# A new order string for the attention and Fourier part of a fused float32 kernel

## The chip, the cores and the metric

The kernel runs on one core of one Trainium2 chip. The metric is the device time of one execution in microseconds; three runs of the kernel before have a median of 1200.18 us (1198.98 to 1201.79). The profile is of one further execution.

The engines are TensorE (PE, matrix products and transposes; its weight loads are shown as PEld), VectorE (DVE), ScalarE (ACT), GpSimd (POOL) and SyncE (SP, which here only issues DMAs). [...]

## The reference

Two blocks follow each other. The first is attention with random features (8 batches, 8 heads, 576 positions, head size 64, 128 features), the second mixes by a Fourier transform and has an MLP:

```python
def phi(x):
    proj = np.einsum('bhsd,md->bhsm', x, omega)
    sq = np.sum(x * x, axis=-1, keepdims=True) / 2.0
    h = proj - sq
    h = h - np.max(h, axis=-1, keepdims=True)
    return np.exp(h) / np.sqrt(m)
q_p, k_p = (phi(q_s), phi(k_s))
kv = np.einsum('bhsm,bhsd->bhmd', k_p, v)
z = np.sum(k_p, axis=2)
num = np.einsum('bhsm,bhmd->bhsd', q_p, kv)
den = np.einsum('bhsm,bhm->bhs', q_p, z)[..., None] + 1e-06
...
X = np.fft.fft(x, axis=1)
X = np.fft.fft(X, axis=2)
u = x + np.real(X)
un = (u - mean(u)) / np.sqrt(var(u) + 1e-06)
ch = np.maximum(un @ w_ch1, 0.0) @ w_ch2
return u + ch
```

Rows are the 8 x 576 = 4608 positions, of width 512; the MLP is 512 to 2048 to 512. The two MLP weights come as float64, everything else as float32.

## The kernel before

The program has two parts, each listed by a call of `listing.run`: the first at L1188, the second at L1514. The change touches the first alone.

**What the first part does.** Attention goes over 32 pairs of heads (`attn`, from L554), three of them in flight. For a pair, SP loads k and q (`kq`, L375 and L378) and v (`vd`, L383). PE transposes `kq` (L504), ACT evicts the transposes (`kqT`, L514), PE multiplies with the features in quarters of its array (L586), DVE takes the maximum (`nmx`, L530), ACT the exponential (`e`, L547). Then PE forms k'v (L620, 36 products), DVE or ACT evicts it (`kv`, L634 or L636), PE transposes the q features (L504 again, with `e`), ACT evicts them (`qeT`, L521), PE multiplies by `kv` (L667, L675), and DVE divides (L684, L685, L696) or ACT does (L692). An L620, L667 or L586 matmul takes PE only 18 to 35 ns, a transpose some 120 ns, so equal times of PE hold very different numbers of instructions.

After four pairs a batch is complete and is mixed (`mix`, from L708): DVE or POOL fold the rows (L723 to L759), PE multiplies by the tables (L779, L789), ACT evicts (`y`, L802), PE multiplies again (L827, L838), ACT, DVE and POOL form the residual sums (L869, L874, L877, L886, L887), and SP stores them in a scratch tensor `us` (L901; a mirrored half goes out by L857 and is copied back by L912, which waits for both L857 transfers to land).

Beside this run the conversion of the weights from float64 (`raw` loads L468 through four buffers; L436 or L438, L441 to L448, L454), the MLP of the first four row tiles (`plain`: norm L951 to L965, first layer L1021, `ht` L1005 or L1007, second layer L1044, L1057) and the sums of weights and rows that the second part needs (L1114, L1172, L1089; stores L1137, L1139).

**What the second part does.** The remaining 4096 rows go through the MLP in eight blocks of 512, with Strassen-like products: L1228 for the first layer, L1407 for the second. The first L1228 starts at 441 us of the profiled execution.

**What sets the order.** Each piece of work is a generator that yields a `Step` (engine or a choice of engines, an assumed duration, what it needs and frees) and then writes its instructions. `Listing.run` (L184) keeps a list `todo` of the pieces whose next step waits to be listed. Without a string it takes the step that its own clock lets begin first. With the string `PICKS` (L63) each character names the place in `todo` to take next:

```python
pick = next(picks, None)
other, n = divmod(DIGITS.index(pick), 36) if pick else (0, 0)
best = None
for item in todo if pick is None else [todo[n]]:
    got = self.start(*item[2:], other=other)
```

A value of 36 or more (a capital letter or a sign) means the place less 36 and, for a step with a choice, the engine that the listing's clock holds for the second best. So the string decides the order of instructions on all five engines at once, and for a few kinds of steps the engine: L436 POOL or L438 ACT, L454, L723, L739, L752, L886 and L1114 POOL or DVE, L634 DVE or L636 ACT, L696 DVE or L692 ACT, L1005 DVE or L1007 ACT. Buffers, loads on SP and PSUM banks follow the order in which steps are listed.

## Time and profile before

| | |
|---|---|
| median of 3 runs | 1200.18 us |
| the profiled execution | 1200.75 us |
| its span, first to last instruction | 1198.9 us |
| PE busy | 1171.2 us |
| first L1228 matmul (second part) | 441.1 us |
| PE busy from 441 us to 1199 us | 752.2 of 758 us |
| PE clock granted, mean | 0.998 |

How to read the lines that follow in the prediction: the slices cut the span into 40 equal stretches of 30 us, with one digit for each, the busy share in tenths. A wait line says engine, what it was to write and its line, what released it, then us in total, how often, and the longest. "issue" means that nothing with a semaphore held the engine. A line of the timeline has start, duration, engine, line, operation and tile shapes, the number of instructions merged, and in brackets the idle time before. A matmul in float32 stands twice in the profile (L620: 36 in the program, 72 in the trace), a transpose once. q1 is the queue of SP's DMAs, q8 and q14 carry instructions.

### The profile page before, as it was taken

The numbers are of one execution on the slowest core, as the hardware profiler recorded it, in microseconds if no ns is written. First come the engines' busy times: TensorE is split into PE (matmuls) and PEld (weight loads), VectorE is DVE, ScalarE is ACT, GpSimd is POOL, SyncE is SP. The second block draws the span as 40 slices with busy tenths as digits, with TensorE's granted clock in tenths as the row PEclk, the third lists the DMA queues.
The fourth block names the chain that finished last, engine by engine and source line by source line (L and its number), as shares of the span: only waits on it lengthen the run. The fifth ranks groups of instructions, "written<-read, shape, count | busy, mean of one in ns | idle before, by whom it ended". The sixth has DMA issues, their size and how long they took to land.

```text
span 1198.9 us, 31843 instructions
## 1 busy us (share of the span) xinstructions
PE 1171.2 (98%) x12753; PEld 1048.6 (87%) x12753; DVE 702.7 (59%) x1479; ACT 488.6 (41%) x1583; POOL 438.0 (37%) x509
## 2 busy tenths in 40 slices
PE   7899899999999999999999999999999999999998
PEld 6777788878969778998998998999899899899898
DVE  5889888896555652572582473374275176266255
ACT  7989889877755212222222222222222222222211
POOL 3355344553565305304314323322421431431421
PEclk9999999999999999999999999999999999999999
DMA  8655845645663332582482384195096086177155
GB/s 254 184 148 179 244 147 176 205 148 181 176 228 134 121 119 104 187 270 80 147 291 100 105 293 139 63 298 177 13 309 195 30 269 197 62 233 242 62 161 192
DMA packets 144740, 205.71 MB, mean 172 GB/s; under 512 B 49104, under 2 KB 58576, under 8 KB 144592
## 3 DMA queue, kind: packets, MB, share of 16 engines
q1 hardware_dynamic: 144224, 203.54, 53.3%
q8 instruction: 101, 1.65, 0.6%
q14 instruction: 47, 0.39, 0.1%
q10 hardware_dynamic: 368, 0.13, 0.0%
HBM read 171.90 MB, written 35.91 MB: 173 GB/s over the span
## 4 chain that ended last, share of the span: by engine, by line
PE 67%; DVE 0%; issue 0%; ACT 0%; DVEq 0%
PE banks L1228 32%; PE banks L1407 29%; PE banks L1044 2%; PE banks L961 1%; PE banks L1021 1%; PE banks L827 0%; PE banks L779 0%; PE banks L667 0%; PE banks L789 0%; PE banks L838 0%; DVE u L957 0%; DVE part L1387 0%; PE banks L675 0%; ACT qeT L521 0%; DVE ur L1339 0%
## 5 line engine op out<-in xcount | busy, mean ns | idle before, releaser
L1214 DVE CUSTOM_DVE_ANT_0 hid<-banks,s 128x256 f32<-128x256 f32 x192 | 79.7, 423 | 255.3 <-PE banks L1228 250.5
L1407 PE MATMUL banks<-wl,sums 128*128 128x128 f32 x1792 | 217.3, 275 | 0.0
L1407 PEld LDWEIGHTS banks<-wl,sums 128*128 128x128 f32 x1792 | 208.8, 192 | 0.4
L1242 ACT ACTIVATE s<-banks 128x256 f32<-128x256 f32 x192 | 73.7, 384 | 261.1 <-PE banks L1228 261.1
L547 ACT ACTIVATE e<-banks,nmx 128x128 f32<-128x128 f32 x576 | 163.5, 449 | 20.4 <-DVE nmx L530 20.1
L1228 PE MATMUL banks<-unT,w 128*128 128x256 f32 x704 | 167.5, 379 | 0.0
L1228 PEld LDWEIGHTS banks<-unT,w 128*128 128x128 f32 x704 | 132.7, 190 | 17.9 <-issue 0.5
L1382 ACT ACTIVATE s<-banks 128x128 f32<-128x128 f32 x168 | 46.7, 278 | 242.3 <-PE banks L1407 195.7
L1228 PE MATMUL banks<-tt,w1s 128*128 128x256 f32 x512 | 126.2, 379 | 0.0
L1295 POOL TENSOR_TENSOR hs<-hid 128x256 f32<-128x256 f32 x64 | 46.4, 725 | 205.6 <-DVE hid L1214 178.9
L1228 PEld LDWEIGHTS banks<-tt,w1s 128*128 128x128 f32 x512 | 97.2, 190 | 13.3
L530 DVE TENSOR_REDUCE nmx<-banks 128x8 f32<-128x1024 f32 (+1 forms) x96 | 89.8, 954 | 30.4 <-PE banks L586 24.0
L1387 DVE TENSOR_TENSOR part<-banks,s 128x128 f32<-128x128 f32 x168 | 48.9, 291 | 88.9 <-PE banks L1407 88.3
L1407 PE MATMUL banks<-wl,hid 128*128 128x128 f32 x768 | 97.6, 275 | 0.0
L1407 PEld LDWEIGHTS banks<-wl,hid 128*128 128x128 f32 x768 | 93.5, 192 | 1.2
L1295 POOL TENSOR_TENSOR hs<-hid,hs 128x256 f32<-128x256 f32 x64 | 46.6, 729 | 120.1 <-issue 95.2
L521 ACT ACTIVATE qeT<-banks 128x256 f32<-128x256 f32 (+1 forms) x192 | 79.2, 593 | 10.7 <-PE banks L504 10.5
L586 PE MATMUL banks<-om,kqT 64*64 64x128 f32 x2304 | 79.8, 277 | 3.6 <-ACT kqT L514 2.7
L1228 PE MATMUL banks<-unT,w1s 128*128 128x256 f32 x320 | 80.7, 379 | 0.0
L955 POOL TENSOR_TENSOR rstd<-rstd,mhalf 128x1 f32<-128x1 f32 x36 | 25.8, 718 | 142.2 <-DVE rstd L953 141.1
L586 PEld LDWEIGHTS banks<-om,kqT 64*64 64x64 f32 x2304 | 64.5, 134 | 14.3 <-ACT kqT L514 4.1
L1407 PE MATMUL banks<-wl,hs 128*128 128x128 f32 x576 | 74.9, 275 | 0.4 <-DVE part L1387 0.4
(125 smaller groups left out, 1993.2 us busy)
## 6 DMA issues: line engine op xcount, KB each, us to landing
wl<-w2l SPq DMA_DIRECT2D x392, 256.0 KB, 3.7
raw<-in_moe_w_ch_dram SPq DMA_DIRECT2D x32, 512.0 KB, 5.4
kq<-in_k_dram SPq DMA_DIRECT2D x32, 288.0 KB, 3.9
kq<-in_q_dram SPq DMA_DIRECT2D x32, 288.0 KB, 4.4
vd<-in_v_dram SPq DMA_DIRECT2D x32, 288.0 KB, 5.0
u<-us SPq DMA_DIRECT2D x36, 256.0 KB, 4.0
ur<-us SPq DMA_DIRECT2D x36, 256.0 KB, 4.4
out_dram<-ur SPq DMA_DIRECT2D x34, 256.0 KB, 2.4
```

The costliest lines, as they stand in the source:

```text
L521: nc.scalar.activation(out=dst[:, i], in_=of, func=AF.Copy)
L530: nc.vector.tensor_reduce(nmx[:, :, 0:num], pps[:, :, 0 : MF * num].rearrange("p b (c m) -> p b c m", m=MF), axis=AX.X, op=ALU.max, negate ...
L547: nc.scalar.activation(out=e[:, c + (i if num == 1 else 0), :], in_=pps[:, i, MF * c : MF * c + MF], func=AF.Exp, bias=nmx[:, i, c : c + 1],)
L586: nc.tensor.matmul(pps[cols, c, MF * m : MF * m + MF], lhsT=kqT[rows, j, cols], rhs=om2[rows, :],)
L955: nc.gpsimd.tensor_tensor(rstd[:], rstd[:], mhalf[:], op=ALU.pow)
L1214: nc.vector._custom_dve(TENSOR_ADD_SAT, out=o, in0=ps, in1=sb, s0=FMAX, s1=0.0)
L1228: nc.tensor.matmul(ps[:, 0:HT], lhsT=left(dc), rhs=right(dc), start=start and dc == 0, stop=(dc == D2 - 1), skip_group_check=True,)
L1242: nc.scalar.activation(out=s[:], in_=ps[:, 0:HT], func=AF.Copy)
L1295: nc.gpsimd.tensor_tensor(out=o, in0=l, in1=r, op=op)
L1382: nc.scalar.activation(out=s[:], in_=ps[:, 0:128], func=AF.Copy)
L1387: nc.vector.tensor_tensor(out=part[:, t, 128 * m : 128 * m + 128], in0=ps[:, 0:128], in1=saved[with_][:], op=ALU.add,)
L1407: nc.tensor.matmul(ps[:, 0:128], lhsT=left[:, f], rhs=wls[j, i, n][:, f], start=start and f == 0, stop=(f == 3), skip_group_check=True,)
```

## The change

`PICKS` is replaced. Both strings have 1851 characters; the first seven are equal, then they part. 131 characters of the old string and 135 of the new one ask for the second-best engine. Nothing else in the file differs: same steps, same buffers, same assumed durations, same second part.

```diff
 PICKS = (
-    "130ddec4dedefddeef0ebe38dfgabbhi08da9h9h9h928ecigh9bcdgghecbdbgiiegbekl88m7jbcagePOIf7cgig8kk7c87i7j"
...
-    "43b2249ac44b8dH97370bFa24G786CD45777777044224032010"
+    "130ddec0dcd3dedefedeef38dfcfcajjji0j88a88i9i9i827fePhjdgfeiddelghkffhjg8cdikfPiijhcddgiceeffghfeifej"
...
+    "ebf7bGdF7G7743695887a0bJI9F887888477773032113021110"
 )
```

In the built programs every engine's order differs from the first microseconds on. PE still has 6737 matmuls and transposes; up to the first L1228 its instructions come in 372 runs of one line instead of 381. Of the choices of engine, these differ between the two programs (instructions in all):

| operation | before | after |
|---|---|---|
| kv copy, L634 DVE / L636 ACT | 13 / 19 | 18 / 14 |
| division, L696 DVE / L692 ACT (ten each) | 26 / 60 | 27 / 50 |
| ht, L1005 DVE / L1007 ACT | 29 / 35 | 32 / 32 |
| weight cast, L438 ACT / L436 POOL | 17 / 15 | 19 / 13 |
| weight sum, L454 DVE / POOL | 5 / 27 | 7 / 25 |
| fold, L723 DVE / POOL | 10 / 6 | 7 / 9 |
| fold, L752 DVE / POOL | 18 / 14 | 24 / 8 |
| residual, L886 DVE / POOL | 10 / 30 | 11 / 29 |
| w2 sums, L1114 DVE / POOL | 13 / 31 | 16 / 28 |

On SP the loads and stores are the same in kind and number, in another order; for instance, between the second batch's mirror stores (L857) and their copy back (L912) stood three `raw` loads and a k load, and now stands one `raw` load.

## The prediction

> **What bounds the kernel now.** I read the page first (busy times, the slices), then what TensorE (PE) waits for, then PE in order of time at its longest wait, then the DMA queues and the stages there.

> ```profile
> PE 1171.2 (98%) x12753; PEld 1048.6 (87%) x12753; DVE 702.7 (59%) x1479; ACT 488.6 (41%) x1583; POOL 438.0 (37%) x509
> PE   7899899999999999999999999999999999999998
> DVE  5889888896555652572582473374275176266255
> ACT  7989889877755212222222222222222222222211
> DMA  8655845645663332582482384195096086177155
> q8 instruction: 101, 1.65, 0.6%
> ```

> PE is the bound: 1171.2 of 1198.9 us. What is not PE lies in the first eight or nine slices of 30 us, where VectorE (DVE) and ScalarE (ACT) are nearly full too. From 385.6 us to the end the chain of waits is PE after PE. So an order of the first part can win only idle time of PE before about 300 us. The stages price it (columns: stretch, length, busy time and count of PE, weight loads, DVE, ACT, POOL, then PE's clock, DMA share, GB/s):

> ```profile
> 0.00:60.00 60.00, 48.13 (x1195) 40.24 (x1199) 41.24 (x68) 49.93 (x167) 21.93 (x24) 1.00 0.76 219
> 60.00:120.00 60.00, 56.27 (x1196) 47.62 (x1190) 52.93 (x122) 53.50 (x179) 32.46 (x32) 1.00 0.56 163
> 140.40:142.90 2.50, 0.01 (x3) 0.00 (x0) 1.47 (x3) 2.50 (x9) 0.88 (x1) 1.00 1.07 370
> 142.90:147.10 4.20, 4.18 (x44) 4.06 (x45) 2.88 (x7) 1.37 (x4) 1.93 (x2) 0.59 0.93 219
> ```

> Idle PE is 11.9 and 3.7 us in the first two rows and 21.9 us up to 300 us (summed over ten such stretches of 30 us). The releasers:

> ```profile
> PE banks L483 <- DMA om<-in_omega_dram: 4.9, 1, 4.9
> PE banks L620 <- issue: 4.2, 3, 2.5
> PE banks L586 <- ACT kqT L514: 2.7, 5, 1.2
> PE banks L667 <- issue: 1.2, 2, 0.8
> PE banks L504 <- issue: 1.1, 3, 0.7
> ```

> 4.9 us are the first load, which no order removes. 6.5 us are "issue": PE waits for nothing that a semaphore shows. The other 10.5 us are waits for ACT and DVE, and gaps too short to be listed. The longest issue wait, in order of time:

> ```profile
> 137.61 1.72 PE L667 MATMUL banks<-kv,qeT 128*64 128x65 f32 x32
> 139.49 0.92 PE L620 MATMUL banks<-vd,e 64*64 64x65 f32 x46
> 142.92 0.96 PE L620 MATMUL banks<-vd,e 64*64 64x65 f32 x26 [2.51 <-issue]
> 143.81 3.50 PE L504 MATMUL banks<-ident,e 128*128 128x128 f32 x18
> ```

> ```profile
> q1 hardware_dynamic: 1190, 1.77, 101.4%
> q8 instruction: 1, 0.02, 1.3%
> ```

> The wait had a sequel: the clock stood at half from 143.14 to 146.56 us (0.59 in the stage row above), so 18 transposes took 3.50 us instead of about 2.3. Half of 3.41 us, 1.7 us, is the price; it is counted as busy.

> [...] the trace has 3.41 us at half after 2.5 us idle, while idles of 1.17 and 1.14 us did nothing.

> **The change part by part.** Only the order string changes. Same matmuls, same second part; only which step goes next, and for a few steps which engine.

> *PE's blocks.* I counted both built orders into blocks of 256 PE instructions and gave them lengths by this trace's rows (L620: 72 in 1.28 us; L667: 32 in 1.15; L586: 40 in 1.32; transposes about 0.12 each). Stalls before, and what I expect after:
> - 132.00 (1.14): the block grows from 3.65 to 4.30 us. Two mirror stores are still in flight: 0.3.
> - 142.92 (2.51): the block before the wait is now 108 L620 and 20 L667 (1.92 + 0.72 = 2.64 us) against 40 L620, 32 L667, 8 L675, 46 L620 (0.71 + 1.15 + 0.40 + 0.82 = 3.08). Shorter, so worse with the same fetch. But the queue differs. Before, SP issued two 512 KB weight loads at 134.65 and the 512 KB copy back at 136.95, just as the block began (136.9), then q and two v loads. After, one weight load instead of three stands between the mirror stores and the copy, and the copy needs only 100.4 us of PE's and 102.6 of DVE's work before it (104.0 and 107.6 before), so it is mostly through when the block begins at 109.8 us of PE work; the next v load waits for a product inside the block. I take a fetch wait of 1.0 us (bounds 0.4 and 3.6): 1.0 + 2.4 - 2.64 = 0.8; bounds 0.2 and 3.4. At 0.8 the clock stays whole.
> - 166.55 (0.57): 2.45 to 3.76 us, gone. 218.99 (0.21): 4.02 to 4.39, gone.
> - 77.12 (0.84), 39.91 and 34.43 (0.87): lengths within 0.15 us, kept: 0.8 and 0.9. 284.82 (0.33): 4.56 to 4.24, so 0.6.
> - New short blocks: 124 L620 and 4 L586 late in the part (2.3 us; the DMA share there is about 0.37 and fetch waits were mostly 0.2 to 0.7): 0.5. One of 2.83 us (3.02 before, hidden in an ACT wait of 1.17) under denser loads: 0.3.

> Sum after: 0.3 + 0.8 + 0.8 + 0.9 + 0.6 + 0.5 + 0.3 = 4.2, against 6.5 + 1.7 = 8.2: a gain of 4.0. With the bounds of the second line (and the clock at the upper end) it is 4.6 to -0.3.

> *Waits for ACT and DVE.* For each PE group I set the PE work between its trigger and its use against the duration of what lies between (a transpose's eviction at 0.66 us, a maximum of 1.2 us and four exponentials, and so on). The missing time, summed, is 24.4 us before and 22.8 after; 10.5 us were real, so 0.7 gained. Bounds: +2 and -2, since 60 to 90 us looks worse (7.8 to 11.3) and 120 to 210 better. ACT has 3.3 us less to do (5 kv copies at 352 ns, 3 ht at 315, 10 x at 218 less; 2 weight casts at 801 more), which I put in the same 0.7. POOL loses some 11 us and is on no chain.

> *Changes of matmul shape* on PE up to the first L1228: 218 before, 212 after. One costs about 0.1 us (8 L675 start 0.33 us before the next transpose, and 8 of them are 0.22): 0.6 gained.

> *Loads.* The closest load that the new order places is a q load 5.6 us of PE work before its use, behind a v load; before, the closest beside the very first were 4.2 to 6.0 and PE never waited for one. q lands in 4.4 us at the median, v in 5.0. I take nothing; if it is late, 1 to 2 us. Queues of ACT, DVE and POOL: their own fetch packets (8 KB) show some 3.5 us of issue waits together, not PE's; nothing.

> *Second part* (441 us on): PE has 752.2 of 758 there and the order isn't touched; its inputs are ready tens of us ahead by the same counting (DVE 53 us instead of 61 at PE's work of 380): nothing.

> Sum: 4.0 + 0.7 + 0.6 = 5.3 us off the profiled execution's own 1200.75 (span 1198.9 and 1.85 around it): 1195.4. That execution is 0.57 above the median of 1200.18, so against the median 1194.9; I say **1195.0**.

> **Rivals.**
> - *The stall stays* (chance 0.20). The two v products stand back to back, and the fetch is as late as before: 3.63 + 2.4 - 2.64 = 3.4 us, and the clock halves, 1.7. That gives back 2.6 + 1.7 of the 5.3: 1199.7. For it: the shorter block. Against it: the copy moved forward.
> - *Quiet throughout* (0.13): all but 1 us of fetch stalls go, 7.2 + 1.3: 1192.2. For it: only eight places to mend. Against it: five of them keep their block lengths.
> - *DVE becomes the bound* (0.22), the slower side. The new engine choices give DVE 8.2 us more in the first part (5 kv copies 1.4, six folds and their copies 3.8, two weight sums 2.0, three w2 sums 2.3, ht, x and bmp 2.7, less three halves 4.0). At 160 us of PE work the order asks DVE to be 5.8 us of work ahead of PE, instead of 2.5. Between 60 and 270 us DVE is busy 52.93 of the second row's 60 and over 25 of every 30 us on to 270: it has 27 us spare, most of it spent waiting for the matmuls it reduces. If none of that takes up the work, 8.2 - 5.3 = 2.9 us slower: 1203.7. It decides once more than 5.3 of the 8.2 us isn't absorbed. Against it: only 3.3 us of the 8.2 fall before the tightest place.

> **How the numbers follow.** Forecast 0.45, rivals 0.20, 0.13, 0.22. A measurement of this kernel tells about 0.2% (2.4 us) from no change. Forecast: 0.42 faster, 0.03 same. First rival: 0.06 faster, 0.14 same. Second: 0.13 faster. Third: 0.02 same, 0.20 slower. Together 0.61, 0.19, 0.20. The range holds the forecast's terms at their bounds and both near rivals, and leaves out half of the third: 1190.5 to 1202.0. The forecast's own range is 1192 to 1198.

> **What would show it.** In the profile after: issue waits of PE near 4 us instead of 6.5, none over 1.5; no stretch at half clock between 100 and 200 us; PE idle before 300 us near 17 us; ACT and DVE releasers together near 10. It is wrong if an issue wait over 2 us and a half clock remain, if DVE rises above 27 of 30 us between 120 and 240 with PE released by L530, L634 or L696 there, or if anything differs after 441 us beyond a shift.

## The result

| | before | after | ratio |
|---|---|---|---|
| median of 20 runs each | 1199.55 us | 1195.11 us | 0.9967, interval 0.9957 to 0.9978 |
| second series (63 and 22 runs) | 1199.39 us | 1195.88 us | 0.9974, interval 0.9966 to 0.9982 |
| profiled execution | 1200.75 us | 1197.48 us, second series 1196.38 us | |

The new order is faster, by 4.4 and 3.5 us of median in the two series. The page of the kernel after (busy times, the slices of 30 us, the instruction queue):

```profile
PE 1171.4 (98%) x12753; PEld 1048.4 (88%) x12753; DVE 704.6 (59%) x1501; ACT 485.0 (41%) x1567; POOL 427.3 (36%) x494
PE   7999999999999999999999999999999999999998
DVE  4888899886655551572572473474275176266255
ACT  6989899868655112222222222222222222222211
q8 instruction: 101, 1.65, 0.6%
```

PE is busy as long as before (1171.2) and idle for less. The stages (stretch, length, busy time and count of PE, weight loads, DVE, ACT, POOL, then PE's clock, DMA share, GB/s):

```profile
0.00:60.00 60.00, 49.31 (x1174) 41.04 (x1174) 41.04 (x68) 48.17 (x161) 20.51 (x24) 0.97 0.70 203
60.00:120.00 60.00, 56.75 (x1194) 48.38 (x1196) 52.93 (x122) 53.21 (x182) 28.01 (x28) 1.00 0.63 183
24.15:27.56 3.41, 3.41 (x51) 2.96 (x51) 1.55 (x4) 0.00 (x0) 0.53 (x1) 0.50 0.58 157
```

The half clock near 143 us is gone, but this execution has one at 24 us, the third row. PE's releasers up to its first L1228:

```profile
PE banks L483 <- DMA om<-in_omega_dram: 5.0, 1, 5.0
PE banks L667 <- issue: 2.6, 2, 1.9
PE banks L586 <- ACT qeT L521: 2.3, 4, 1.2
PE banks L504 <- ACT e L547: 1.5, 5, 0.4
PE banks L620 <- issue: 1.3, 1, 1.3
PE banks L675 <- issue: 0.7, 1, 0.7
```

And the place that held the stop of 2.51 us before, in order of time:

```profile
138.13 0.80 PE L667 MATMUL banks<-kv,qeT 128*64 128x65 f32 x18
139.64 0.62 PE L667 MATMUL banks<-kv,qeT 128*64 128x65 f32 x14 [0.72 <-issue]
```

PE still stops inside a product (18 of 32 matmuls of L667), at the same place of the 256-instruction count, but for 0.72 us. A second profile of the same kernel has no half clock in the first part; its issue waits:

```profile
PE banks L667 <- issue: 2.1, 2, 1.2
PE banks L620 <- issue: 1.8, 2, 1.3
PE banks L675 <- issue: 1.2, 1, 1.2
```

Where the time came from, up to the first L1228 (idle is that moment less PE's busy time before it):

| us | before | after | after, second profile |
|---|---|---|---|
| first L1228 starts | 440.9 | 437.9 | 436.8 |
| PE idle until then | 22.0 | 18.9 | 19.3 |
| of it the first load | 4.9 | 5.0 | 5.0 |
| of it issue | 6.5 | 4.6 | 5.1 |
| of it ACT, DVE, late loads and short gaps | 10.6 | 9.3 | 9.2 |
| PE busy until then | 418.9 | 419.1 | 417.5 |
| stretch at half clock | 3.41, at 143 us | 3.41, at 24 us | none |

The second profile's gain of 4.1 us is 1.3 of issue, 1.4 of the other waits, and 1.4 of busy time, where the half clock was. The 9.2 us hold 0.6 us in which PE waited for k loads. After the first L1228 nothing changed: 758.0, 757.7 and 757.7 us to the end of the span.

### The profile page after: what moved, and what is told of

Read it like the earlier page. It is cut to its first block, busy times and chain, and to the rows that moved or that the text cites. A ratio compares the mean times of both kernels' runs of the same rounds, so it can differ in the third digit from the quotient of the medians.

```text
span 1195.6 us, 31831 instructions
## 1 busy us (share of the span) xinstructions
PE 1171.4 (98%) x12753; PEld 1048.4 (88%) x12753; DVE 704.6 (59%) x1501; ACT 485.0 (41%) x1567; POOL 427.3 (36%) x494
## 3 DMA queue, kind: packets, MB, share of 16 engines
q8 instruction: 101, 1.65, 0.6%
## 4 chain that ended last, share of the span: by engine, by line
PE 88%; ACT 9%; DVE 1%; issue 1%; DMA 0%; ACTq 0%; DVEq 0%
PE banks L1228 32%; PE banks L1407 29%; PE banks L1021 5%; PE banks L1044 5%; ACT e L547 4%; PE banks L586 4%; PE banks L504 4%; ACT qeT L521 3%; PE banks L667 2%; PE banks L620 2%; PE banks L827 2%; PE banks L961 1%; PE banks L779 1%; ACT kqT L514 1%; PE banks L789 1%
## 5 line engine op out<-in xcount | busy, mean ns | idle before, releaser
L547 ACT ACTIVATE e<-banks,nmx 128x128 f32<-128x128 f32 x576 | 163.3, 453 | 21.9 <-DVE nmx L530 21.7
L1228 PE MATMUL banks<-unT,w 128*128 128x256 f32 x704 | 167.5, 379 | 0.0
L1228 PEld LDWEIGHTS banks<-unT,w 128*128 128x128 f32 x704 | 132.7, 190 | 17.9 <-issue 0.5
L1228 PE MATMUL banks<-tt,w1s 128*128 128x256 f32 x512 | 126.2, 379 | 0.0
L1228 PEld LDWEIGHTS banks<-tt,w1s 128*128 128x128 f32 x512 | 97.3, 190 | 13.2
L530 DVE TENSOR_REDUCE nmx<-banks 128x8 f32<-128x1024 f32 (+1 forms) x96 | 89.4, 952 | 22.8 <-PE banks L586 21.7
L521 ACT ACTIVATE qeT<-banks 128x256 f32<-128x256 f32 (+1 forms) x192 | 82.6, 584 | 14.6 <-PE banks L504 14.1
L586 PE MATMUL banks<-om,kqT 64*64 64x128 f32 x2304 | 80.3, 279 | 3.0 <-ACT qeT L521 2.3
L1228 PE MATMUL banks<-unT,w1s 128*128 128x256 f32 x320 | 80.7, 379 | 0.0
L586 PEld LDWEIGHTS banks<-om,kqT 64*64 64x64 f32 x2304 | 64.6, 135 | 14.2 <-issue 5.2
```

Of the source, the lines that this page charges most:

```text
L521: nc.scalar.activation(out=dst[:, i], in_=of, func=AF.Copy)
L530: nc.vector.tensor_reduce(nmx[:, :, 0:num], pps[:, :, 0 : MF * num].rearrange("p b (c m) -> p b c m", m=MF), axis=AX.X, op=ALU.max, negate ...
L547: nc.scalar.activation(out=e[:, c + (i if num == 1 else 0), :], in_=pps[:, i, MF * c : MF * c + MF], func=AF.Exp, bias=nmx[:, i, c : c + 1],)
L586: nc.tensor.matmul(pps[cols, c, MF * m : MF * m + MF], lhsT=kqT[rows, j, cols], rhs=om2[rows, :],)
L1228: nc.tensor.matmul(ps[:, 0:HT], lhsT=left(dc), rhs=right(dc), start=start and dc == 0, stop=(dc == D2 - 1), skip_group_check=True,)
```

## The experiments

Theory 1: the issue waits are PE waiting for its own next block of 256 instructions. Their size is the time that the block's packet starts late, plus about 2.4 us (an estimate from the kernel before: the packet that starts at 140.55 us takes 1.04 us, and PE goes on 1.33 us after its end), less the work in the block before. By this theory they depend on where block boundaries fall in the order, and on transfers at that moment. Theory 2: they are waits for operands, buffers, ACT or DVE that the trace can't name, and the new order gains because of its better spacing of those. Each ratio is to executions of the kernel before that were timed beside it; the medians are of 5 to 22 executions.

**Moving the boundaries.** Products that nobody reads, ahead of PE's first transposes, where PE waits for its first load. Each is four PE instructions (two matmuls and two weight loads in the trace), so 16, 48 and 64 of them move every boundary by 64, 192 and 256 instructions. Order, waits and buffers stay.

```diff
+        for i in range(16):
+            q = slice(D * (i % 2), D * (i % 2) + D)
+            nc.tensor.matmul(omps[q, 256:257], lhsT=ident[q, q], rhs=ident[q, 0:1])
         nc.tensor.transpose(omps[:, 0:128], om2d, ident[:])
```

The kernel before, moved by 64:

> The kernel before with 16 one-column products (64 PE instructions) ahead of everything, in the time in which PE waits for its first load. Order, buffers and data are those of before; only the grid of 256-instruction blocks lies 64 instructions earlier in the work. Theory 1 (instruction fetch): with a fetch wait of 2 us the blocks of the first part are short by 19.0 us in sum instead of 13.5, so the 8.2 us of fetch stalls and half clock of before should become 10 to 13: slower by 2 to 5 us, and issue waits at other places. Theory 2 (the stops come from data or buffers, and the gain of the new order from ACT and DVE): same places, same time within 1 us.

By 192:

> The same with 48 products (192 PE instructions). Theory 1: the blocks are short by 8.6 us instead of 13.5, so faster by 2 to 4 us, with the long stop near 142.9 us gone or much shorter and no half clock there. Theory 2: no change within 1 us.

By 256, a whole block, as the control:

> The same with 64 products (256 PE instructions): the grid falls on the same instructions as in before, with one block more. A control for what the extra products do by themselves. Theory 1: the same time within 1.5 us (the start of PE may lose up to 1 us[...]) and the stops at the same matmuls as before. Theory 2: no change either.

| kernel before with | median | ratio | first kv product later by |
|---|---|---|---|
| 64 more | 1202.30 | 1.0023, 1.0011 to 1.0035 | 0.6 us earlier |
| 192 more | 1200.21 | 1.0008, 0.9999 to 1.0017 | 1.6 us |
| 256 more | 1202.43 | 1.0027, 1.0017 to 1.0037 | 3.8 us |

The times were half hits. 64 came within its expectation, but its profile is of an execution of 1197.77 us and has 4.6 us of stops at block boundaries and no half clock; so it shows where the stops are, and not what made the median 2.8 us slower. The other two start later, by more than I had allowed for. If that delay passes on in full, which isn't shown, both are some 0.9 us under the kernel before without it, and that isn't the gain that theory 1 expected of 192. The places are what counts. First the control, in order of time, then 64:

```profile
140.87 0.92 PE L620 MATMUL banks<-vd,e 64*64 64x65 f32 x46
145.21 1.13 PE L620 MATMUL banks<-vd,e 64*64 64x65 f32 x26 [3.42 <-issue]
```

```profile
137.04 0.46 PE L620 MATMUL banks<-vd,e 64*64 64x65 f32 x14
138.25 1.14 PE L620 MATMUL banks<-vd,e 64*64 64x65 f32 x58 [0.75 <-issue]
```

Moved by a whole block, PE stops after the same 46 of 72 matmuls as before. Moved by 64, it stops after 14: 32 matmuls with their 32 weight loads earlier, which is 64 instructions. No operand can explain that. With 192 the stop stands in the transposes behind that product:

```profile
142.92 1.58 PE L504 MATMUL banks<-ident,e 128*128 128x128 f32 x13 [2.05 <-ACT w L438]
```

It is listed as released by ACT's weight cast L438, which no transpose of that group reads, and it ends 1.56 us after the block's packet; a name on a stop is no proof.

The new order, moved by 64:

> The changed kernel with 16 one-column products, 64 instructions of TensorE, ahead of its first transposes, where it waits for the first load anyway; they moved the first kv product by less than 0.1 us in the kernel before. Order and waits are otherwise the same; every boundary of an instruction block now lies 64 instructions earlier in the program. Theory 1: the new order was searched for one position of the boundaries, so the stops move to other matmuls and grow: at a fetch wait of 2.0 us the sum of the blocks' shortfalls is 17.7 us instead of 13.7 (a relative measure, not a time), and in the kernel before a rise from 13.5 to 19.0 cost 2.8 us; time +1 to +4 us against the changed kernel, 1196 to 1199. Theory 2: no operand and no buffer comes at another time, so the same within 0.5 us.

It took 1203.05 us (ratio 1.0031, 1.0020 to 1.0042): slower than the kernel before, and 7.2 us slower than the same order without the 16 products, more than I expected. The stop of the last section went from L667 back into L620:

```profile
135.90 2.85 PE L620 MATMUL banks<-vd,e 64*64 64x65 f32 x130
140.25 0.46 PE L620 MATMUL banks<-vd,e 64*64 64x65 f32 x14 [1.50 <-issue]
```

14 matmuls of L620 and 18 of L667 earlier: again 32, and 64 instructions. In this profile the first L1228 starts at 442.36 us instead of 436.83; the stops at block boundaries sum to some 7.9 us (6.4 listed as issue, and one of 1.49 us at 61 us that is listed under L438 and ends 1.38 us after its packet) instead of 5.1 in the second profile, and a half clock of 3.41 us, a price of 1.7, follows the one at 61 us. That is some 4.5 of the 5.5 us; 0.7 more is in waits for ACT (7.9 us instead of 7.2). Moved by 64, the new order (1203.05 us) is no faster than the old one (1202.30 us). So the gain of the new order is tied to one position of the boundaries. The 1.4 us of other waits that it also gained in the second profile have no experiment of their own.

**Changing the transfers.** In the kernel before, three 512 KB transfers were queued ahead of the block that stops at 142.92 us. The first try moved the loads of `raw` 17 and 18 behind the two v loads, and the conversion of `raw` 17, which could not stay ahead of its load; PE's order is the same.

```diff
 SP    raw<-in_moe_w_ch  (16)
-SP    raw<-in_moe_w_ch  (17, 18)
 SP    us<-uh, kq<-in_q, vd<-in_v, vd<-in_v
+SP    raw<-in_moe_w_ch  (17, 18)
 ...
-DVE   L441, L443, L446, L448, L454 of raw 17 as before
+DVE   L441, L443, L446, L448, L454 of raw 17 later
```

> The kernel before with two of its 512 KB weight loads moved behind the two v loads that follow the copy back of the second batch (and the conversion of one of them behind the products, so that nobody waits for it). PE's order and its blocks are exactly those of before. Theory 1: the fetch for the block at 137 us starts 0.5 to 1.5 us after the block begins instead of 3.6, so the stop of 2.5 us shrinks to under 0.8 and the half clock goes: faster by 2 to 4 us. Theory 2: PE's stop stays, within 1 us of before.

It took 1205.12 us, 1.0046 (1.0033 to 1.0058). PE at the target, and 20 us later:

```profile
140.92 0.92 PE L620 MATMUL banks<-vd,e 64*64 64x65 f32 x46
142.21 0.68 PE L620 MATMUL banks<-vd,e 64*64 64x65 f32 x26 [0.37 <-issue]
...
157.56 1.30 PE L586 MATMUL banks<-om,kqT 64*64 64x128 f32 x34
162.90 0.70 PE L586 MATMUL banks<-om,kqT 64*64 64x128 f32 x6 [4.04 <-DVE ht L1005]
```

At the target theory 1 was right: in the packet records the fetch started 1.66 us after PE entered the block before, instead of 3.68, and the stop shrank from 2.51 to 0.37 us, with the clock whole. But the conversion, moved, now stood on DVE's queue ahead of an eviction:

```profile
159.92 2.72 DVE L454 TENSOR_TENSOR w<-w,raw 128x512 f32<-128x512 f32 x1
162.57 0.28 DVE L1005 TENSOR_SCALAR ht<-banks 128x128 f32<-128x128 f32 x1
```

PE waited 4.04 us for that PSUM bank and the clock stood at half for 6.83 us. This is the kind of wait that theory 2 means, and here it was made by hand. So a cleaner try: one load (`raw` 18) behind the v loads, all else in order.

> The kernel before with one load of 512 KB (raw 18) issued on SP's queue behind the two v loads that follow it, and nothing else: all other engines have the same order, which the first try at a quiet window had not kept. Theory 1: the instruction block used at 142.9 us is fetched with 512 KB less ahead of it; its fetch wait falls from 3.6 us to between 1.7 and 3.0, its stop from 2.5 us to between 0.5 and 1.9[...]; time -0.7 to -3.5 us against the kernel before. Theory 2 (operands and buffers): only the v loads come some 1 to 1.5 us earlier and raw 18 later; the stop of 2.5 us keeps its length within 0.3, and the time is the same within 0.5 us unless raw 18's conversion is late.

1198.05 us, 0.9989 (0.9981 to 0.9998). The time is in the range, but not for the stated reason:

```profile
140.78 0.68 PE L620 MATMUL banks<-vd,e 64*64 64x65 f32 x26 [2.00 <-issue]
```

The fetch wait went from 3.68 to 3.26 us only, the stop from 2.51 to 2.00, both outside what theory 1 expected, and the half clock stayed. The first L1228 came 2.3 us earlier in its profile, most of it from other stops and waits. That is inconclusive for the size of the effect.

The opposite on the kernel after: two more transfers, ahead of the copy back, over the block that is used at 140 us. They copy weights to a scratch tensor that nobody reads.

```diff
+            for n in range(2 if b == 1 else 0):
+                nc.sync.dma_start(junk[n], w1v[:, n, 0:CV].bitcast(U32))
             nc.sync.dma_start(*(a.rearrange("p (i d) -> i p d", i=16) for a in (ahead, back)))
```

> The changed kernel with two more transfers of 512 KB, from memory to memory, on SP's queue just ahead of the second batch's copy back (L912), so that transfers lie over the block that is used at 140 us; nothing reads what they write, and TensorE's order is the same. Theory 1: the fetch wait of that block rises from 1.6 us to between 3 and 4, its stop from 0.7 us to between 2 and 3.4[...]; time +2 to +5 us against the changed kernel. Theory 2: the stop stays at 0.7 us or less, since no operand of TensorE comes by these transfers; what could come late are the kq and v loads of later pairs, named in the waits as released by DMA, and without these the time is the same within 1 us.

The kernel after alone, timed beside it:

> The changed kernel once more, for a second profile and for the time beside the next three. Both theories: 1194.5 to 1196.5 us, 3.0 to 5.0 below the kernel before. Theory 1 (the stops of TensorE are waits for its own instruction blocks of 256 instructions) expects the stops at the same places of the instruction order as in the first profile (the blocks used at 24, 63, 140 and 371 us), with sizes that differ by some tenths; the large one at 24 us, with a fetch wait of 4.9 us and a half clock behind it, may be smaller, since that profile was taken at 1197.5 us and most executions lie near 1195. Theory 2 (waits for operands and buffers that the trace puts down as issue) expects the same time and has no opinion on the places.

It took 1195.88 us, with the stops in the places expected, one more of 0.50 us at 134.69 us, and 0.88 us instead of 1.87 at the first. With the transfers 1197.01 us (0.9982, 0.9974 to 0.9990), 1.1 us slower: the stop is in the expected range, the fetch wait and the time are below it, and no half clock followed. The place, in order of time:

```profile
136.63 0.80 PE L667 MATMUL banks<-kv,qeT 128*64 128x65 f32 x18
139.58 0.63 PE L667 MATMUL banks<-kv,qeT 128*64 128x65 f32 x14 [2.15 <-issue]
```

The same matmul, and 2.15 us instead of 0.72 and 1.18; nothing is named as late. The data queue from 136.0 to 139.5 us (packets, MB, share of the 16 engines), with the transfers and then in the first profile of the kernel after:

```profile
q1 hardware_dynamic: 1909, 1.12, 108.2%
```

```profile
q1 hardware_dynamic: 1573, 0.72, 76.7%
```

The fetch wait was 2.65 us here, 1.61 and 1.53 in the two profiles without. Two more kernels that keep this part of the order, the next one and the one with the swap at 59 us, had waits of 1.81 and 1.03 us and stops of 0.85 and 0.20. So the stop with the transfers is longer than in any of four profiles without, and no operand of PE comes by them; theory 2 has no account of it. It is one profile, though, and far from the transfers, at 34.66 us, it has another stop of 1.62 us that neither profile of the kernel after has. Nor does the share of the data queue alone set the wait: between PE's entry into the block before and the start of the packet it was 94% with the transfers, and 89% and 22% in the two profiles without, whose waits are alike.

**Giving the blocks more work.** If, as theory 1 has it, a stop is fetch less work, a slow group between two products of small matmuls removes it. At 371 us, a block of the new order is 124 small matmuls long:

```diff
 L620 x36
+L1021 x4
 L620 x36
-L1021 x4
 L504
```

> The changed kernel with one swap in TensorE's order at 371 us: the projection group L1021 x4 that follows two adjacent kv products (L620, 2 x 36) goes between them. Nothing else is moved but what hangs on the second product. Theory 1: the instruction block that was 124 small matmuls with 1.97 us of work now holds 1.0 us of L1021 as well, 2.8 to 2.9 us; its stop falls from 1.3 us to 0.3 to 0.6, time -0.7 to -1.0 us against the changed kernel. Theory 2: the stop is a wait for an operand or a buffer of the second product, and with one microsecond of other work ahead of it it falls too, but the product then waits for the eviction of the first product's buffer on ScalarE, a wait with ACT as its releaser of up to 0.5 us; time -0.5 to +0.3.

First the kernel after (second profile), then with the swap:

```profile
366.87 2.02 PE L620 MATMUL banks<-vd,e 64*64 64x65 f32 x123
370.21 0.57 PE L620 MATMUL banks<-vd,e 64*64 64x65 f32 x21 [1.32 <-issue]
```

```profile
367.56 1.16 PE L1021 MATMUL banks<-unT,w 128*128 128x128 f32 x8
368.65 0.91 PE L620 MATMUL banks<-vd,e 64*64 64x65 f32 x43
369.75 0.69 PE L620 MATMUL banks<-vd,e 64*64 64x65 f32 x29 [0.19 <-issue]
```

1.32 became 0.19 us, and no wait for ACT took its place. In its profile the first L1228 starts 1.3 us earlier (435.56). The median, 1196.01 us (0.9973, 0.9961 to 0.9984), is the same: one microsecond is less than ten executions resolve.

Two more swaps of the kind, at 59 and at 137 us, first together with this one:

```diff
+L779 x4, L789 x2
 L667 x16, L675 x4        (59 us)
-L779 x4, L789 x2
...
+L504 x5
 L667 x16, L675 x4        (137 us)
-L504 x18
+L504 x13
```

> The changed kernel with the swap at 371 us (L1021 x4 between the two kv products) and two more of its kind: five transposes (L504) go ahead of the product L667, L675 at 137 us, and the frequency products L779, L789 go ahead of L667, L675 at 59 us. Theory 1: the blocks with the stops of 1.3, 1.2 and 1.3 us (371, 138 and 61 us in the second profile) hold 1.0, 0.5 and some 1 us of work more; the stop at 371 goes to 0.2, those at 138 and 61 fall by 0.5 to 1.0 each; time -1.5 to -3 us against the changed kernel, ratio to the kernel before 0.9950 to 0.9962. Theory 2: the order of work is not limited by instructions, and the products that now come later delay their evictions on VectorE (rden, x) by 0.6 and 2 us, which the transposes and later pairs wait for; time 0 to +2 us against the changed kernel.

It was slower: 1198.60 us, 0.9989 (0.9979 to 1.0000). Its profile has only 0.5 us of stops at block boundaries left, and yet:

```profile
64.12 0.66 PE L504 MATMUL banks<-ident,kq 128*128 128x128 f32 x4 [0.80 <-ACT x L692]
65.15 0.66 PE L504 MATMUL banks<-ident,kq 128*128 128x128 f32 x4 [0.37 <-ACT x L692]
...
138.45 0.66 PE L504 MATMUL banks<-ident,e 128*128 128x128 f32 x4 [1.44 <-ACT e L547]
```

The stop of 1.25 us at 61 us (second profile) has become two waits for ACT of 1.17 together, and that of 1.18 at 138 one of 1.44. The stage shows why (columns as above):

```profile
133.40:139.40 6.00, 4.35 (x165) 3.48 (x164) 5.90 (x11) 6.00 (x21) 3.05 (x2) 1.00 0.64 166
```

ACT is busy for all 6.00 us and DVE for 5.90, so in this order PE has to wait there even when its instructions are at hand. In the kernel after (second profile) ACT is as full up to the end of the stop, 5.84 of 5.84 us from 132.60 to 138.44, so that stop of 1.18 us cost little by itself. To see which swap costs, each alone with the one at 371 us. At 59 us:

> The last kernel without the transposes ahead of L667 at 137 us: the changed kernel with the swaps at 371 us and at 59 us alone. Theory 1: the stop at 61 us (0.7 to 1.3 us) goes and nothing takes its place at 138, where the stop of 0.7 to 1.2 us comes back: 1194.5 to 1195.5 us, that is 0.4 to 1.4 below the changed kernel. Theory 2: the last kernel's profile shows in place of the stop at 61 us two waits for x on ScalarE (0.8 and 0.4 us), since L675 ends later and ten evictions (L692, 2.16 us) hang on it; so the swap at 59 us gains nothing, 1195.5 to 1197, and if these waits are what made the last kernel slow, 1198 or more.

At 137 us:

> The last kernel without the frequency products ahead of L667 at 59 us: the changed kernel with the swaps at 371 us and at 137 us alone. Theory 1: 1194.5 to 1195.5 us, the stop at 138 us gone and the one at 61 us there again. Theory 2: the stop at 138 us comes back as a wait of the moved transposes for the exponentials of ScalarE (1.4 us in the last kernel's profile, where ScalarE works on evictions and exponentials without a pause from 133.4 to 139.4 us); if that wait is longer in other executions and brings the half clock, this kernel carries most of the last one's loss against the changed kernel: 1197.5 to 1199.

With 59 us: 1195.88 us (0.9977, 0.9968 to 0.9987), the same as the kernel after, with the two waits for ACT in the profile (0.80 and 0.36). With 137 us: 1196.93 us (0.9982, 0.9973 to 0.9991), with the wait for ACT of 1.44. Neither shows a gain, and the loss of both together is more than the sum of the two: against the kernel before, timed beside each, both together gain 1.1 us of median, 59 alone 3.5 and 137 alone 2.4, where the kernel after gains 3.5. These differences are near what so few executions resolve. The profile of the kernel with both was taken in the shortest of its executions (1195.81 us) and doesn't show what the longer ones did. This stays open. None of these kernels is shown to beat the kernel after.

## Why the prediction was right, and where not

**The time.** 1195.0 us was forecast, 1195.11 and 1195.88 came. Part of that is luck: I took 5.2 us off a median of 1200.18, and the larger samples put the kernel before at 1199.4 to 1199.6. The gain was 4.4 and 3.5 us. All my terms together were too large by one to two microseconds. And the sum of issue, 4.2 forecast and 4.6 and 5.1 measured, is right by luck, as the table shows: places forecast at 2.9 us in all had 0 and 0.5 us, and 2.6 and 2.1 us came at two places that I had not foreseen.

**PE's blocks.** The runs bear theory 1 out in kind: boundaries moved by 64 instructions moved the stops by 64, two loads out of the way shortened one (2.51 to 0.37 us), added work shortened another (1.32 to 0.19), and with added transfers one was longer (2.15 us instead of 0.72 and 1.18), in one profile. The sizes were less good:

| place (predicted) | first profile | second profile |
|---|---|---|
| 132.00 (0.3) | none | 0.50 |
| 142.92 (0.8, clock whole) | 0.72, whole | 1.18, whole |
| 166.55 and 218.99 (gone) | gone | gone |
| 77.12, 39.91 and 34.43 (0.8 and 0.9) | none | none |
| 284.82 (0.6) | none | none |
| late block of 124 L620 (0.5) | 1.32 | 1.32 |
| block of 2.83 us (0.3) | none | none |
| not foreseen, 24 and 63 us | 1.87 and 0.72 | 0.88 and 1.25 |
| sum (4.2) | 4.6 | 5.1 |

The step that failed is "lengths within 0.15 us, kept": I took the fetch waits of before as belonging to the place. They don't. By the packet records the three blocks did keep their lengths (within 0.1 us), but their packets started 0.18, 1.27 and 0.73 us after PE entered the block before (34.43, 39.91 and 77.12) instead of 1.96, 2.94 and 1.91, and no stop was left. In the new order the packets of the first 60 us started 4.91 and 2.90 us after PE entered the block before (3.96 and 3.49 in the second profile) at 24 and 63 us, where other loads now lie. The late block was sized with a fetch wait of 0.2 to 0.7 and had 1.21 and 0.95. At 142.92 I took 1.0, and 1.61 and 1.53 came: with the prediction's own sum that makes stops of 1.4 and 1.3. The second profile has 1.18; in the first, a wait for ACT of 0.47 us inside the block took part of it, and 0.72 remained. Nor did the copy back decide it: until the packet started, the data queue was nearly empty in the second profile (22% busy, 89% in the first), and the wait was the same. What sets these waits stays open. The clock stayed whole, which carried 1.7 us of the sum. In the first profile that 1.7 was given back at 24 us. The eight stops of before end 1.29 to 1.48 us after their packets, not 1.3 to 1.4, which changes none of these sums.

**Waits for ACT and DVE.** 0.7 was forecast, 1.3 and 1.4 came, within the bounds, though 0.2 and 0.6 us of what is left are late loads. **Matmul shapes.** The 0.6 isn't seen: with a half clock of 3.41 us in both, busy time is 419.1 us in the first profile and 418.9 before, and in the second, without one, it fell by 1.4 where the half clock alone, estimated at half of its 3.41 us, gives 1.7. **Loads and second part.** Nothing, as forecast, beside 0.2 us of PE waiting for a q load in the first profile and 0.6 for k loads in the second.

**The rivals.** The stall didn't stay; with two more transfers it reached 2.15 us, without a half clock, so the rival's size of 3.4 us needs more than that. Quiet throughout was not reached. Against it I said that five places keep their block lengths; my own list has three, and just these three fell quiet. DVE didn't become the bound: it was busy 247.6 and 248.3 us up to 300 us, 5 to 6 more than before (242.5), but up to the first L1228 only 2.1 and 1.1 us more, not the 8.2 of the rival, and PE waited for it less. But the swaps show that the rival was near: where the stops are filled, PE waits for ACT, with DVE nearly full beside it at 138 us.

**What would show it.** Issue near 4 us (4.6, 5.1), none over 1.5 (the first profile has 1.87), no half clock between 100 and 200 us (none), PE idle before 300 us near 17 (17.2 and 17.7), ACT, DVE and short gaps near 10 (9.3, 9.2): all but one.

## What to carry to other kernels

A stop of an engine in the middle of one product, with nothing named, is worth counting in instructions before looking for a late operand: here 64 instructions put ahead moved the stop by 64, from behind 46 of 72 matmuls to behind 14. The gain of an order that is tuned to such boundaries can hang on its instruction count; here 16 idle products ahead turned a gain of 3.5 us into a loss of 3.7. And before filling such a stop, see whether ACT and DVE are full beside it: with ACT busy for all 6.00 and DVE for 5.90 of 6.00 us, the stop of 1.18 us at 138 us became a wait for ACT of 1.44.

## What the runs showed of the hardware

- A block's packet started late by very different times in these traces, and the share of the data queue until then didn't settle it. At the place of the long stop it was 1.53 us at 22% and 1.61 at 89% (kernel after, second and first profile), 1.66 at 63% (two loads moved), 2.65 at 94% (added transfers), 3.68 at 100% (kernel before) and 4.50 at 91% (kernel before moved by 256). In the first 25 us of the new order moved by 64 it was 5.0 us.
- The length of one stop didn't settle whether the clock was at half behind it. It was after stops of 1.49 (new order moved by 64), 1.83 and 4.04 (two loads moved), 1.87 (first profile after), 2.00 (one load moved), 2.51 (kernel before) and 3.42 us (kernel before moved by 256). It was not after 1.50 and 1.68 (new order moved by 64), 1.62 and 2.15 (added transfers) and 2.05 us (kernel before moved by 192). It lasted 3.41 us, or 6.83 after the stops of 3.42 and 4.04.
- In the profile of the kernel before and the first of the kernel after, PE was idle for 2.51 and 2.00 us of the 3.41 us just ahead of the half clock. In any 3.41 us before or behind that, from the first full clock (at 10.0 and 10.5 us) to the end of PE's work, it was at most 1.17 and 1.32 us. What decides isn't shown: with the added transfers, no half clock came after the stop of 2.15 us.
- The kernel after has its large stops mostly at the same places in two profiles, but not with the same lengths: they differ by up to 1.0 us (1.87 and 0.88 at 24 us), and one of 0.50 us is in the second profile alone. The start of a fetch differs by more: for the block that PE enters at 34 to 36 us it was 0.18 and 0.38 us after entry into the block before in the two profiles, and 3.34 us, with the stop of 1.62, in the kernel with added transfers, which has the same instructions up to there. The 22 times of the second series spread over 6 us (1193.81 to 1199.97); part of that is likely these stops and the half clock behind them, which was not tried.
- One weight sum (L454) on DVE took 2.72 us beside a POOL fold (L723) of 2.87 us (two loads moved, at 159.92 us); the twelve in the profiles of the kernels before and after took 0.68 to 1.67 us.
